# Turning C and two token blocks of x by transposing transfers on SP's queue, in place of VectorE's and TensorE's turnings

## Chip, cores and metric

The kernel runs on one core of a Trainium2 chip, in bfloat16 with float32 accumulation. The metric is the device time of one execution in microseconds (us), lower being better. The core has TensorE (PE, with its weight loads listed as PEld), VectorE (DVE), ScalarE (ACT), GpSimd (POOL) and SyncE (SP). SP computes nothing here: it issues transfers, which sixteen DMA engines carry out.

## What is computed

A gate mixes a state-space layer and a small feed-forward block over the same 2,048 tokens of 448 features. Cut to what matters:

```python
g = sigmoid((x * gate_w).sum(-1, keepdims=True))
# a: a complex diagonal recurrence over the tokens, state size 448
Lam_bar = exp(dt * Lam);  B_bar = ((Lam_bar - 1.0) / Lam)[:, None] * Bmat
Bu = einsum("bld,pd->blp", x, B_bar)
h[t] = Lam_bar * h[t - 1] + Bu[t]
a = 2.0 * einsum("blp,dp->bld", h, C_re + 1j * C_im).real + x * Dskip
# b: silu(x @ w1) @ w2, 448 -> 1792 -> 448
b = silu(x @ w1) @ w2
out = g * a + (1 - g) * b
```

TensorE contracts over the partitions (the 128 rows of on-chip memory), so three inputs that lie the other way round in DRAM have to be turned: x (tokens by features, needed as features by tokens), B, and C (outputs by states, needed as states by outputs).

## The kernel before

**Tiling.** The tokens are cut into four chunks of 512 (`tc` 0 to 3) and sixteen blocks of 128 (`tb` 0 to 15). The turned x stands in `xT[:, tc, q, :]` with four column groups `q` that start at features 0, 128, 256 and 320 (`XCOL`, the last two overlapping by 64). Each chunk goes through these products on PE: `F(tc)`, fourteen tiles x·w1 (line 711, weights `w1s`); `B(tc)`, seven tiles x·B (line 711, weights `BT`); `G(tb)`, the second feed-forward product (`ffn2`, line 822); and `C(tb)`, the read-out of the recurrence (`readout`, line 843, weights `CP`). F and B tiles go in pairs that hold two of the eight PSUM banks until ACT (lines 681 and 690) or DVE (line 688) has evicted them.

**The recurrence.** `lanes(tc)` runs on DVE: a rotation by COS and SIN, seven scans (line 784), a copy of the scans by POOL transfers, and a rotation back. The rotation back writes two products into `PO` (`"PO0"`, `"PO1"`) and leaves the result in `H[tc % 3]`, which `C` reads.

**Order.** PE runs in program order, which the bottom of the kernel writes by hand. For all other queues the class `Plan` simulates the program with costs and priorities given at each operation and fixes an order, so a planned cost sets an order and not a time. SP is one such queue: its transfers and the waits before them are carried out one after another in the planned order. `Waits` then places semaphore waits by the names that each operation reads and writes.

**How x is turned.** Chunk 0 is turned by PE at the start (line 504). For chunks 1, 2 and 3 `x_transposes` (line 536) lets PE turn the natural copy `xnat` with 32 small matmuls of 64 rows each into two banks; ACT and DVE (chunk 1) or ACT alone (chunks 2 and 3) copy the result into `xT` (lines 544 and 546). `x_blocks` is another way, by DVE, which `XBLK = ()` leaves unused.

**How C is turned.** `load_C` loads C by six transfers into `Cnat`, which lies in the buffer of `H[2]`, after POOL has zeroed a quarter of it (line 462). `readout_columns` turns 32 by 32 blocks on DVE (line 870, four instructions) into `UG[2]`, and sixteen transfers on SP (line 876) put the blocks where they belong in `CP`. Later `readout_weights(k)` scales these columns: two ACT copies with a scale into `ct` and two DVE instructions back into `CP` for k = 0 to 2 (lines 885, 886, 891, 894), and for the half-filled k = 3 two ACT copies of 64 partitions and one DVE instruction. `CTAT = 59.0` tells the planner not to place the ACT part earlier than that.

**Who evicts.** `UDVE = (0, 1, 4, 5, 6)` names the B tiles of chunk 0 that DVE evicts; ACT takes the pair (2, 3). `OUTA = tuple(range(4, 12))` names the blocks whose read-out is evicted by ACT into `ct` (line 848), added to `xnat` by a POOL transfer (line 850) and stored from there (line 851). The other blocks are evicted by one DVE instruction into one of five tiles `ot` (line 853) and stored from there (line 856).

**SP's queue at the start.** In planned order: x chunk 0, w1, B, the rest of w1, `gwb`, `dkb`, x chunk 1, the six loads of C, w2, x chunks 2 and 3, then the sixteen transfers of C's blocks; after these only stores.

The hand-written order of PE, which the steps below refer to:

```python
x_products(F(0, 0, NH) + B(0) + F(0, NH) + B(1), {..., XT1K: xt(1, XT1), 8: [lambda: lanes(0)] + [readout_columns] + ...}, [K - 2])
... G(0, 1, 2, 3) ... cp(0, 1, 2, 3)
x_products(F(1) + F(2, 0, 1) + B(2), {2: xt(2, "aa")} if 2 not in XBLK else {})
... G(4, 5, 6, 7)
x_products(F(2, 1) + B(3) + F(3), {1: xt(3, "aa") if 3 not in XBLK else [], 9: [lambda: gates(3)]})
C(0..3), lanes(3), C(4..7), G(8..13), C(8..11), G(14, 15), C(12..15)
```

Of the kernel before, what the change touches and what calls it, by code (L numbers as in the profile page):

```python
# [7 lines left out]
ALU = mybir.AluOpType  # L8
AF = mybir.ActivationFunctionType
# [20 lines left out]
XPRIO = {2: 15, 3: 20.2}  # L30
XBLK = ()
XBEH = {2: "PI_0", 3: "H0_0"}
UDVE = (0, 1, 4, 5, 6)
OUTA = tuple(range(4, 12))
PRMF = (1, 0)
PRMP = 9.7
CPRIO = 2.9
# [3 lines left out]
CBEH = ""  # L41
# [257 lines left out]
def bass_gated_mix__ssm_conv_s5__dense_activation_silu__prompt_kernel(nc, A_x, A_Lambda_re, A_Lambda_im, A_B_re, A_B_im, A_C_re, A_C_im,  # L299
               A_log_dt, A_Dskip, B_x, B_w1, B_w2, gate_w, out):  # L300
    with ExitStack() as ctx:
# [3 lines left out]
        def sb(name, shape, dtype):  # L305
            return E(nc.sbuf_tensor(name, list(shape), dtype))
# [15 lines left out]
        Cnat = H[2][:, :, :].rearrange("p s n -> p (s n)").rearrange("p (b l) -> p b l", b=4)  # L322
        cnn = [f"H2_{s}" for s in range(7)]
# [9 lines left out]
        ot = [sb(f"ot{k}", [128, D_MOD], BF16) for k in range(NOT)]  # L333
        ones = nc.const_aps.tensor(1.0, [128, 512], BF16)
# [40 lines left out]
        def sem():  # L375
            _s[0] += 1
            return E(nc.semaphore(name=f"d{_s[0]}"))
# [10 lines left out]
        def act_cost(n, aps=0):  # L388
            return 0.17 + n * 0.000833 + 0.09 * aps
# [4 lines left out]
        def ACT(fn, r, w, cost, prio, tag=""):  # L394
            return P.add("act", fn, r, w, cost, prio, tag=tag)

        def DVE(fn, r, w, cost, prio, tag=""):
            return P.add("dve", fn, r, w, cost, prio, tag=tag)

        def POOL(fn, r, w, cost, prio=10, tag=""):  # L400
            return P.add("pool", fn, r, w, cost, prio, tag=tag)
# [6 lines left out]
        def load(q, dst, src, name, nbytes, prio=None, after=()):  # L408
            nl[0] += 1
            prio = nl[0] if prio is None else prio  # L410
            P.add(q, lambda e: e.dma_start(dst, src), list(after), name.split(), 0.6 if q == "pool" else 0.5 if nbytes > 2000 else 0.35, prio, sem(), nbytes, tag="ld " + name)  # L411
# [32 lines left out]
        for dst, src, name in ((gwb, gate_w, "gwb"), (dkb, A_Dskip, "dkb")):  # L444
            load("sp", dst[:, :], src.rearrange("(o n) -> o n", o=1).partition_broadcast(128).rearrange("p o n -> p (o n)"),
                 name, 128 * 896)

        def load_xn(tc):
            load("sp", xnat[:, 4 * tc:4 * tc + 4, :],
                 x2[tc * CH:(tc + 1) * CH, :].rearrange("(b p) d -> p b d", p=128), f"xn{tc}", CH * 896)  # L450

        def load_C():

            n = 0
            for b0, b1, p in ((0, 3, 128), (3, 4, 64)):
                rows = lambda a: a[128 * b0:128 * b0 + p * (b1 - b0), :].rearrange("(b p) l -> p b l", p=p)
                for dst, src in (((0, 448), rows(A_C_re)), ((512, 896), rows(A_C_im[:, 0:384])), ((448, 512), rows(A_C_im[:, 384:448]))):
                    load("sp", Cnat[0:p, b0:b1, dst[0]:dst[1]], src, f"Cn{n}" + (" " + " ".join(cnn) if n == 0 else ""),
                         p * (b1 - b0) * max(300, 2 * (dst[1] - dst[0])), None, ["Cnz"] * b0)
                    n += 1  # L460

        POOL(lambda e: e.memset(Cnat[:, 3, :], 0.0), [], ["Cnz"], 0.9, 5)
        load_xn(1)
        load_C()
        load("sp", w2s[:, :, :], B_w2.rearrange("(fb p) d -> p fb d", p=128), "w2", F_FF * 896)
        load_xn(2)
# [55 lines left out]
        for tc in XBLK:  # L522
            xn_of[tc] = {q: [f"xT{tc}_{g}{m}" for g in range(4) for m in range(4)] for q in range(4)}
# [23 lines left out]

        def x_blocks(tc):


            X32 = (xT[:, 3, :, :] if tc == 2 else H[2][:, 0:4, :]).rearrange("p m (q b i) -> p m q b i", q=4, i=32)
            names = [f"XT{tc}2_{k}" for k in range(4)]
            held = cnn if tc == 3 else xn_of[3][0]
            xs = xnat[:, 4 * tc:4 * tc + 4, :]
            for k, (q0, q1, c, b0, b1) in enumerate(((0, 3, 0, 0, 2), (0, 3, 0, 2, 4), (3, 4, XCOL[3], 0, 2), (3, 4, XCOL[3], 2, 4))):
                n = q1 - q0
                src = xs[:, b0:b1, c:c + 128 * n].rearrange("p b (q m i) -> p b q m i", q=n, i=32)
                dst = X32.rearrange("p m q b i -> p b q m i")[:, b0:b1, q0:q1, :, :]
                DVE(lambda e, dst=dst, src=src: e.transpose(dst, src), [f"xn{tc}"] + names[0:k][0:1], [names[k]] + cnn * (tc == 3 and k == 0), 0.15 + 256 * n / 960, XPRIO[tc], "xTd")
            k = sem()  # L560
            for g in range(4):
                for m in range(4):
                    to = xT[32 * m:32 * m + 32, tc, :, :].rearrange("p q (b g i) -> p (q b) g i", b=4, i=32)[:, :, g, :]
                    P.add("sp", lambda e, to=to, g=g, m=m: e.dma_start(to, X32[32 * g:32 * g + 32, m, :, :, :].rearrange("p q b i -> p (q b) i")),
                          names + held, [f"xT{tc}_{g}{m}"], 0.68, 400, k, 150000, tag="xTm")
# [293 lines left out]
        ctn = [f"CT{g}{m}" for g in range(4) for m in range(4)]  # L859

        def readout_columns():

            C32 = UG[2][:, 0:NSLOT, :].rearrange("p s n -> p (s n)").rearrange("p (m t b i) -> p m t b i", m=4, b=4, i=32)
            names = [f"X32_{k}" for k in range(4)]
            held = [f"U2_{s}" for s in range(7)] + ["U2_3i"]
            turned = [f"BT{s}_{h}" for s in range(7) for h in range(2)]
            for b in range(4):
                src = Cnat[:, b, :].rearrange("p (t m i) -> p t m i", m=4, i=32)
                dst = C32.rearrange("p m t b i -> p b t m i")[:, b, :, :, :]
                DVE(lambda e, dst=dst, src=src: e.transpose(dst, src), [f"Cn{n}" for n in range(6)] + ["Cnz"] + [CBEH] * (CBEH != "") + cnn + turned, [names[b]],  # L870
                    0.15 + 896 / 960, CPRIO, "CTd")
            k = sem()
            for g in range(4):
                for m in range(4):
                    to = CP[32 * m:32 * m + 32, :, :].rearrange("p t (b g i) -> p (t b) g i", b=4, i=32)[:, :, g, :]
                    P.add("sp", lambda e, to=to, g=g, m=m: e.dma_start(to, C32[32 * g:32 * g + 32, m, :, :, :].rearrange("p t b i -> p (t b) i")),
                          names + held, [f"CT{g}{m}"], 0.75, 400, k, 300000, tag="CTm")

        def readout_weights(k):

            re, im = CP[:, k, 0:D_MOD], CP[:, 4 + k, 0:D_MOD] if k < 3 else None
            c, cn = ct[k % 2], f"ct{k % 2}"
            both = [cn + "a"]
            if k < 3:
                ACT(lambda e: e.activation(c[:, 0, :], im, AF.Copy, scale=sc2[:, k:k + 1]), ctn + ["sc2"], [cn + "a"], act_cost(448, 1), 8, "ct").at = CTAT
                ACT(lambda e: e.activation(c[:, 1, :], re, AF.Copy, scale=sc2[:, k:k + 1]), ctn + ["sc2"], [cn + "b"], act_cost(448, 1), 8, "ct").at = CTAT
                both.append(cn + "b")
            else:
                for a, b in ((slice(0, 64), slice(64, 128)), (slice(64, 128), slice(0, 64))):
                    ACT(lambda e, a=a, b=b: e.activation(c[a, 0, :], CP[b, 3, 0:D_MOD], AF.Copy, scale=sc2[b, 3:4]), ctn + ["sc2"], [cn + "a"], act_cost(448, 1), 8, "ct").at = CTAT  # L890
            DVE(lambda e: e.scalar_tensor_tensor(re, re, sc1[:, k:k + 1], c[:, 0, :], ALU.mult, ALU.add),
                ctn + ["sc1"] + both, [f"CP{k}"], 0.68, CPP, "CP")
            if k < 3:
                DVE(lambda e: e.scalar_tensor_tensor(im, im, nsc1[:, k:k + 1], c[:, 1, :], ALU.mult, ALU.add),
                    ctn + ["sc1"] + both, [f"CP{4 + k}"], 0.68, CPP, "CP")
# [20 lines left out]
        def xt(tc, who):  # L916
            return [lambda: x_transposes(tc, who)]
# [7 lines left out]
        def C(*tbs):  # L925
# [6 lines left out]
                   {PRMF: [parameters], (K - 2, 0): turn_b[:1], K - 2: turn_b[1:2], K - 1: turn_b[2:], XT1K: xt(1, XT1), 8: [lambda: lanes(0)] + [readout_columns] + [lambda tc=tc: x_blocks(tc) for tc in XBLK]}, [K - 2])  # L932
# [7 lines left out]
        x_products(F(1) + F(2, 0, 1) + B(2), {2: xt(2, "aa")} if 2 not in XBLK else {})  # L940
# [4 lines left out]
        x_products(F(2, 1) + B(3) + F(3), {1: xt(3, "aa") if 3 not in XBLK else [], 9: [lambda: gates(3)]})  # L945
# [40 lines left out]
```

## Time and profile before

| what | us |
|---|---|
| median of 3 runs (lowest, highest) | 140.45 (140.28, 141.47) |
| the profiled execution, device time | 140.08 |
| the profiled execution, span from first to last instruction | 138.3 |
| POOL busy | 46.4 |
| last PE instruction of the chain ends, from the span's start | 134.15 |
| mean granted TensorE clock | 0.998 of full speed |

The profile is of one execution; its times count from its first instruction. "Busy" is the time that an engine had an instruction running. The chain of waits follows the work that ended last back to its releaser at each step, so what stands in it sets the end. A group row gives a line, an engine, an operation, the shapes, the count, the total busy time and the mean in ns. The device time holds 1.8 us that lie outside the span.

### The profile page before, as it was taken

To read this page: it belongs to the slowest core of one execution; us is meant where nothing else is said; L and a number is where in the kernel's file an instruction comes from. 1 tells how busy PE (TensorE), PEld (TensorE's weight loads), DVE (VectorE), ACT (ScalarE), POOL (GpSimd) and SP (SyncE) were. 2 spreads that over 40 slices of the span, in tenths; PEclk is the share of its full clock that TensorE was granted. 3 is DMA by queue.
4 is the path that set the end of the run, shared out by engine and by line. 5 is a ranking of instruction groups with operands and counts; after the bars stand their busy time and mean duration, and the time that the engine had idled before them with its cause. 6 is when DMAs were issued, how large, how long until landed. Compare 5 with 4: busy or idle time off the path is not lost.

```text
span 138.3 us, 2881 instructions
## 1 busy us (share of the span) xinstructions
PE 134.7 (97%) x1137; PEld 66.0 (48%) x1137; DVE 119.3 (86%) x160; ACT 96.2 (70%) x167; POOL 46.4 (34%) x81
## 2 busy tenths in 40 slices
PE   7999999999999999999999999999999999999991
PEld 2545454445545444455454444445555555555561
DVE  0319999999999999999999999999999999992053
ACT  3259895999647999998299999899643149752200
POOL 7433030300548603067360030724063404374310
PEclk9999999999999999999999999999999999999999
DMA  4999999477859920029654010475459421379542
GB/s 140 324 355 292 270 364 341 63 102 83 96 77 155 158 40 19 24 37 160 93 87 64 0 38 0 65 120 81 114 106 159 102 33 18 51 100 151 118 102 68
DMA packets 33220, 16.48 MB, mean 119 GB/s; under 512 B 17075, under 2 KB 33078, under 8 KB 33206
## 3 DMA queue, kind: packets, MB, share of 16 engines
q0 software_dynamic: 7216, 6.43, 31.6%
q1 hardware_dynamic: 25440, 9.51, 25.8%
q10 hardware_dynamic: 550, 0.36, 0.8%
q8 instruction: 9, 0.15, 0.4%
q14 instruction: 5, 0.04, 0.1%
HBM read 7.11 MB, written 1.84 MB: 65 GB/s over the span
## 4 chain that ended last, share of the span: by engine, by line
PE 96%; DVE 1%; issue 0%; DVEq 0%
PE ps L711 46%; PE ps L822 31%; PE ps L843 14%; PE ps L489 2%; DVE ot L853 1%; PE ps L536 1%; PE ps L504 1%; PE ps L651 1%; PE ps L490 0%; PE ps L583 0%; PE ps L723 0%; DVEq L293 0%
## 5 line engine op out<-in xcount | busy, mean ns | idle before, releaser
L711 PE MATMUL ps<-xT,w1s 64*128 64x512 bf16 x392 | 48.2, 376 | 0.0
L822 PE MATMUL ps<-w2s,aT 128*128 128x448 bf16 x224 | 43.0, 353 | 0.0
L681 ACT ACTIVATE aT<-ps 128x1024 bf16<-128x1024 f32 (+1 forms) x30 | 28.9, 977 | 10.2 <-PE ps L711 10.1
L822 PEld LDWEIGHTS ps<-w2s,aT 128*128 128x128 bf16 x224 | 21.8, 98 | 20.9 <-issue 0.8
L711 PEld LDWEIGHTS ps<-xT,w1s 64*128 64x128 bf16 x392 | 19.6, 94 | 22.5 <-issue 1.2
L711 PE MATMUL ps<-xT,BT 64*128 64x512 bf16 x196 | 25.8, 376 | 0.0
L784 DVE TENSOR_TENSOR_SCAN Gf<-rc,gin,H 128x512 f32<-128x512 f32 x21 | 25.4, 1265 | 0.1
L830 POOL DMA_DIRECT2D xnat<-fe x16 | 14.4, 922 | 31.2 <-ACT fe L828 23.0
L843 PE MATMUL ps<-CP,H 128*128 128x448 bf16 (+2 forms) x126 | 21.7, 332 | 0.0
L411 POOL DMA_DIRECT2D UG<-Gf x27 | 15.7, 660 | 15.7 <-DVE Gf L784 15.4
L828 ACT ACTIVATE fe<-ps,g 128x448 bf16<-128x448 f32 x16 | 9.9, 627 | 11.1 <-PE ps L822 8.1
L843 PEld LDWEIGHTS ps<-CP,H 128*128 128x128 bf16 x126 | 11.6, 98 | 10.0 <-DVE xnat L752 0.4
L711 PEld LDWEIGHTS ps<-xT,BT 64*128 64x128 bf16 x196 | 10.8, 94 | 11.2 <-DVE Gf L609 0.2
L752 DVE TENSOR_TENSOR H<-UG,COS 128x3584 bf16<-128x3584 bf16 (+2 forms) x9 | 16.1, 1810 | 0.0
L411 POOL DMA_DIRECT2D UG<-UG x8 | 4.5, 567 | 27.1 <-ACT UG L690 27.1
L690 ACT ACTIVATE UG<-ps 128x1024 bf16<-128x1024 f32 (+1 forms) x13 | 11.8, 936 | 0.5 <-PE ps L711 0.5
L853 DVE SCALAR_TENSOR_TENSOR ot<-ps,g,xnat 128x448 bf16<-128x448 f32 (+2 forms) x10 | 5.7, 584 | 7.5 <-issue 6.2
L913 ACT ACTIVATE xnat<-xnat,g 128x448 bf16<-128x448 bf16 x16 | 9.7, 663 | 0.1
L906 ACT ACTIVATE junk<-xg 128x448 bf16<-128x448 bf16 x16 | 9.6, 598 | 0.1
L850 POOL DMA_DIRECT2D xnat<-ct x8 | 6.9, 864 | 6.7 <-ACT ct L848 6.6
L848 ACT ACTIVATE ct<-ps,g 128x448 f32<-128x448 f32 x8 | 5.1, 633 | 5.7 <-PE ps L843 5.7
L752 DVE TENSOR_TENSOR PI<-UG,SIN 128x1536 bf16<-128x1536 bf16 (+1 forms) x8 | 8.5, 1083 | 0.0
(99 smaller groups left out, 123.8 us busy)
## 6 DMA issues: line engine op xcount, KB each, us to landing
UG<-Gf POOLq DMA_DIRECT2D x21, 128.0 KB, 2.8
xnat<-fe POOLq DMA_DIRECT2D x16, 112.0 KB, 2.6
w2s<-in_B_w_dram SPq DMA_DIRECT2D x1, 1568.0 KB, 8.5
xnat<-in_A_x_dram SPq DMA_DIRECT2D x3, 448.0 KB, 8.2
CP<-UG SPq DMA_DIRECT2D x16, 56.0 KB, 2.4
xnat<-ct POOLq DMA_DIRECT2D x8, 112.0 KB, 2.9
out_dram<-xnat SPq DMA_DIRECT2D x8, 112.0 KB, 2.3
out_dram<-ot SPq DMA_DIRECT2D x7, 112.0 KB, 1.8
```

Of the source, the lines that this page charges most:

```text
L411: P.add(q, lambda e: e.dma_start(dst, src), list(after), name.split(), 0.6 if q == "pool" else 0.5 if nbytes > 2000 else 0.35, prio, sem() ...
L681: ACT(lambda e, src=src, dst=dst: e.activation(dst, src(), AF.Silu), [tk, "tbl"], [f"aT{tc % 2}_{m}" for m in names], act_cost(512 * n), 2 ...
L690: ACT(lambda e, src=src, dst=dst: e.activation(dst, src(), AF.Copy), [tk], after, act_cost(512 * n), 5, "U")
L711: r = pe.matmul(bk(toks[k], b), weights(tile, p0, p0 + 64, i), xT[p0:p0 + 64, tc, i, :], start=(h == 0 and n == 0), stop=(h == 1 and n == 2))
L752: DVE(lambda e: e.tensor_tensor(o, a, b, op), r, w, dve_cost(n, 2), prio, tag)
L784: DVE(lambda e, s=s, b=b, init=init: e.tensor_tensor_scan(Gf[:, s, :], rc[:, b:b + 1].to_broadcast([128, CH]), A[:, s, :], init, ALU.mult, ...
L822: r = pe.matmul(bk(tk)[:, 0:D_MOD], aT[tc % 2][:, fb, o:o + 128], w2s[:, fb, :], start=(fb == 0), stop=(fb == NFB - 1))
L828: ACT(lambda e: e.activation(f[:, :], bk(tk)[:, 0:D_MOD], AF.Copy, scale=g1[:, tb:tb + 1]), [tk, f"g1_{tc}"], [fn], act_cost(448, 1), 7, "fe")
L830: P.add("pool", lambda e: e.dma_start(Tb[:, tb, :], f[:, :], accum_op=ALU.add), [fn, f"Tb{tb}"], [f"Tb{tb}"], 0.94, 2, sem(), 250000, tag= ...
L843: r = pe.matmul(bk(tk)[:, 0:b - a], H[tc % 3][:, s, o:o + 128], CP[:, s, a:b], start=(s == 0), stop=(s == NSLOT - 1))
L906: ACT(lambda e, tb=tb, b=b: e.activation(junk[:, :], xg[:, b, :], AF.Copy, accum_out=zl[:, tb:tb + 1]), ["xg"], ["junk", f"zl{tc}"], act_c ...
L913: ACT(lambda e, tb=tb: e.activation(Tb[:, tb, :], xnat[:, tb, :], AF.Copy, scale=g[:, tb:tb + 1]), [f"xd{tc}", f"g_{tc}"], [f"Tb{tb}"], ac ...
```

## The change

C's four pieces and x's chunks 2 and 3 are written turned, straight from DRAM, by `dma_start_transpose` on SP's queue. `load_C`, `readout_columns`, the zeroing of `Cnat`, `x_blocks` and the PE turnings of chunks 2 and 3 go; the natural copies of x stay, since the gates read them. `turn_x(2)` and `turn_C` stand in SP's queue behind w2 and ahead of the natural loads of chunks 2 and 3; `turn_x(3)` waits for the name `"PO1"`, which `lanes(0)` writes. C's last columns are no longer packed into the two halves of `CP[:, 3, :]`: the imaginary part goes to a tile of its own, `C3`, which is the fifth `ot` tile, and `readout_weights(3)` combines the halves with two DVE instructions. `UDVE` gains the pair (2, 3), so DVE evicts all of chunk 0's B tiles, and `OUTA` shrinks to blocks 8 to 11, so DVE evicts the read-outs 4 to 7.

```diff
-XPRIO = {2: 15, 3: 20.2}
-XBLK = ()
-UDVE = (0, 1, 4, 5, 6)
-OUTA = tuple(range(4, 12))
+XDMA = (2, 3)
+XAFT = ["PO1"]
+UDVE = (0, 1, 2, 3, 4, 5, 6)
+OUTA = (8, 9, 10, 11)
...
+        C3, c3n = ot[NOT - 1], " ".join(f"ot{NOT - 1}{m}" for m in range(3))
...
+        def turn(dst, src, name, nbytes, cost, after=()):
+            nl[0] += 1
+            P.add("sp", lambda e: e.dma_start_transpose(dst, src), list(after), name.split(), cost, nl[0], sem(), nbytes, tag="ldT " + name)
+
+        def turn_x(tc, after=()):
+            for c, n in ((0, 3), (3, 1)):
+                turn(xT[:, tc, c:c + n, :], x2[tc * CH:(tc + 1) * CH, XCOL[c]:XCOL[c] + 128 * n], " ".join(f"xT{tc}_{q}" for q in range(c, c + n)), CH * 256 * n, 2.6 if n == 3 else 1.3, after)
+
+        def turn_C():
+            for k, a in enumerate((A_C_re, A_C_im)):
+                turn(CP[:, 4 * k:4 * k + 3, 0:D_MOD], a[:, 0:384], " ".join(f"CT{4 * k + m}" for m in range(3)), 448 * 768, 1.5)
+                turn((CP[:, 3, 0:D_MOD], C3[:, :])[k][:, None, :], a[:, 320:448], "CT3" if k == 0 else c3n, 448 * 256, 1.6)
...
-        POOL(lambda e: e.memset(Cnat[:, 3, :], 0.0), [], ["Cnz"], 0.9, 5)
-        load_xn(1)
-        load_C()
+        if 1 not in XDMA:
+            load_xn(1)
         load("sp", w2s[:, :, :], B_w2.rearrange("(fb p) d -> p fb d", p=128), "w2", F_FF * 896)
+        if 2 in XDMA:
+            turn_x(2)
+        turn_C()
...
         load_xn(2)
         load_xn(3)
...
         def readout_weights(k):
...
+            up = slice(64, 128)
             if k < 3:
...
+                re, im, rn, mn = CP[:, k, 0:D_MOD], CP[:, 4 + k, 0:D_MOD], f"CT{k}", f"CT{4 + k}"
+                a, to = slice(0, 128), ((CP[:, k, 0:D_MOD], re, sc1, [f"CP{k}", rn], 0), (CP[:, 4 + k, 0:D_MOD], im, nsc1, [f"CP{4 + k}", mn], 1))
             else:
...
+                re, im, rn, mn = CP[up, 3, 0:D_MOD], C3[up, :], "CT3", c3n
+                a, to = up, ((CP[0:64, 3, 0:D_MOD], re, nsc1, ["CP3"], 0), (CP[up, 3, 0:D_MOD], im, sc1, ["CP3", rn], 1))
...
+            for dst, src, f, w, n in to:
+                DVE(lambda e, dst=dst, src=src, f=f, n=n: e.scalar_tensor_tensor(dst, src, f[a, k:k + 1], c[a, n, :], ALU.mult, ALU.add),
+                    ([rn] if n == 0 else mn.split()) + ["sc1", cn + "ab"[n]], w, 0.68, CPP, "CP")
...
-                   {..., XT1K: xt(1, XT1), 8: [lambda: lanes(0)] + [readout_columns] + [lambda tc=tc: x_blocks(tc) for tc in XBLK]}, [K - 2])
+                   {..., XT1K: xt(1, XT1) if 1 not in XDMA else [], 8: [lambda: lanes(0)] + [lambda: turn_x(3, XAFT)] * (3 in XDMA and bool(XAFT))}, [K - 2])
...
-        x_products(F(1) + F(2, 0, 1) + B(2), {2: xt(2, "aa")} if 2 not in XBLK else {})
+        x_products(F(1) + F(2, 0, 1) + B(2), {2: xt(2, "aa")} if 2 not in XDMA else {})
...
-        x_products(F(2, 1) + B(3) + F(3), {1: xt(3, "aa") if 3 not in XBLK else [], 9: [lambda: gates(3)]})
+        x_products(F(2, 1) + B(3) + F(3), {1: xt(3, "aa") if 3 not in XDMA else [], 9: [lambda: gates(3)]})
```

More of the change, by code (lines that the diff above doesn't have):

```diff
@@ L29 @@
 XT1 = "da"
-XPRIO = {2: 15, 3: 20.2}
-XBLK = ()
-XBEH = {2: "PI_0", 3: "H0_0"}
-UDVE = (0, 1, 4, 5, 6)
-OUTA = tuple(range(4, 12))
+XDMA = (2, 3)
+XAFT = ["PO1"]
+UDVE = (0, 1, 2, 3, 4, 5, 6)
+OUTA = (8, 9, 10, 11)
 PRMF = (1, 0)
 PRMP = 9.7
-CPRIO = 2.9
 CPP = 20.5
@@ L40 @@
 GPR = (14, 20.3, 21.5, 19)
-CBEH = ""
 CASTB = (360000, 360000, 360000)
@@ L321, in bass_gated_mix__ssm_conv_s5__dense_activation_silu__prompt_kernel @@
         H = [sb(f"H{k}", [128, NSLOT, CH], BF16) for k in range(3)]
-        Cnat = H[2][:, :, :].rearrange("p s n -> p (s n)").rearrange("p (b l) -> p b l", b=4)
-        cnn = [f"H2_{s}" for s in range(7)]
         COS = sb("COS", [128, NSLOT, CH], BF16)
@@ L443, in bass_gated_mix__ssm_conv_s5__dense_activation_silu__prompt_kernel, with load_xn @@
         load_w1("sp", len(w1cuts) - 2, 2, 4)
+        def load_xn(tc):
+            load("sp", xnat[:, 4 * tc:4 * tc + 4, :],
+                 x2[tc * CH:(tc + 1) * CH, :].rearrange("(b p) d -> p b d", p=128), f"xn{tc}", CH * 896)
+        def turn(dst, src, name, nbytes, cost, after=()):
[8 more added lines that the diff above has]
+                turn((CP[:, 3, 0:D_MOD], C3[:, :])[k][:, None, :], a[:, 320:448], "CT3" if k == 0 else c3n, 448 * 256, 1.6)
+        if 1 in XDMA:
+            turn_x(1)
         for dst, src, name in ((gwb, gate_w, "gwb"), (dkb, A_Dskip, "dkb")):
@@ L446, in bass_gated_mix__ssm_conv_s5__dense_activation_silu__prompt_kernel @@
                  name, 128 * 896)
[L448 to L460, printed above, removed]
-        POOL(lambda e: e.memset(Cnat[:, 3, :], 0.0), [], ["Cnz"], 0.9, 5)
-        load_xn(1)
-        load_C()
-        load("sp", w2s[:, :, :], B_w2.rearrange("(fb p) d -> p fb d", p=128), "w2", F_FF * 896)
+        if 1 not in XDMA:
+            load_xn(1)
+        load("sp", w2s[:, :, :], B_w2.rearrange("(fb p) d -> p fb d", p=128), "w2", F_FF * 896)
+        if 2 in XDMA:
+            turn_x(2)
+        turn_C()
+        if 3 in XDMA and not XAFT:
+            turn_x(3)
+        if 1 in XDMA:
+            load_xn(1)
         load_xn(2)
@@ L521, in bass_gated_mix__ssm_conv_s5__dense_activation_silu__prompt_kernel @@
         xn_of = {tc: {q: [f"xT{tc}_{h}" for h in range(2)] for q in range(4)} for tc in range(1, NCH)}
-        for tc in XBLK:
-            xn_of[tc] = {q: [f"xT{tc}_{g}{m}" for g in range(4) for m in range(4)] for q in range(4)}
+        for tc in XDMA:
+            xn_of[tc] = {q: [f"xT{tc}_{q}"] for q in range(4)}
         xn_of[0] = {q: [f"xT0_{q}{part}{h}" for part in range(2) for h in range(2)] for q in range(4)}
@@ L546, in x_transposes @@
                     ACT(lambda e, src=src, dst=dst: e.activation(dst, src(), AF.Copy), [tk], [f"xT{tc}_{h}"], act_cost(1024), 2.2, "xTe")
[L548 to L565, printed above, removed]
         cosn = [f"COS{k}" for k in range(4)] + ["COSd"]
@@ L857, in readout @@
                       [f"ot{tb % NOT}{n}"], [], 0.3, 1, outs[tb % NOT], 128 * 2 * (b - a), tag="st")
[L859 to L877, printed above, removed]
@@ L879, in readout_weights @@
         def readout_weights(k):
-            re, im = CP[:, k, 0:D_MOD], CP[:, 4 + k, 0:D_MOD] if k < 3 else None
             c, cn = ct[k % 2], f"ct{k % 2}"
-            both = [cn + "a"]
+            up = slice(64, 128)
             if k < 3:
-                ACT(lambda e: e.activation(c[:, 0, :], im, AF.Copy, scale=sc2[:, k:k + 1]), ctn + ["sc2"], [cn + "a"], act_cost(448, 1), 8, "ct").at = CTAT
-                ACT(lambda e: e.activation(c[:, 1, :], re, AF.Copy, scale=sc2[:, k:k + 1]), ctn + ["sc2"], [cn + "b"], act_cost(448, 1), 8, "ct").at = CTAT
-                both.append(cn + "b")
-            else:
-                for a, b in ((slice(0, 64), slice(64, 128)), (slice(64, 128), slice(0, 64))):
-                    ACT(lambda e, a=a, b=b: e.activation(c[a, 0, :], CP[b, 3, 0:D_MOD], AF.Copy, scale=sc2[b, 3:4]), ctn + ["sc2"], [cn + "a"], act_cost(448, 1), 8, "ct").at = CTAT
@@ L891, in readout_weights @@
[L891 to L895, printed above, removed]
+                re, im, rn, mn = CP[:, k, 0:D_MOD], CP[:, 4 + k, 0:D_MOD], f"CT{k}", f"CT{4 + k}"
+                a, to = slice(0, 128), ((CP[:, k, 0:D_MOD], re, sc1, [f"CP{k}", rn], 0), (CP[:, 4 + k, 0:D_MOD], im, nsc1, [f"CP{4 + k}", mn], 1))
+            else:
+                re, im, rn, mn = CP[up, 3, 0:D_MOD], C3[up, :], "CT3", c3n
+                a, to = up, ((CP[0:64, 3, 0:D_MOD], re, nsc1, ["CP3"], 0), (CP[up, 3, 0:D_MOD], im, sc1, ["CP3", rn], 1))
@@ new lines, in readout_weights @@
+            ACT(lambda e: e.activation(c[a, 0, :], im, AF.Copy, scale=sc2[a, k:k + 1]), mn.split() + ["sc2"], [cn + "a"], act_cost(448, 1), 8, "ct").at = CTAT
+            ACT(lambda e: e.activation(c[a, 1, :], re, AF.Copy, scale=sc2[a, k:k + 1]), [rn, "sc2"], [cn + "b"], act_cost(448, 1), 8, "ct").at = CTAT
+            for dst, src, f, w, n in to:
+                DVE(lambda e, dst=dst, src=src, f=f, n=n: e.scalar_tensor_tensor(dst, src, f[a, k:k + 1], c[a, n, :], ALU.mult, ALU.add),
+                    ([rn] if n == 0 else mn.split()) + ["sc1", cn + "ab"[n]], w, 0.68, CPP, "CP")
@@ L931, in bass_gated_mix__ssm_conv_s5__dense_activation_silu__prompt_kernel @@
         x_products(F(0, 0, NH) + B(0) + F(0, NH) + B(1),
-                   {PRMF: [parameters], (K - 2, 0): turn_b[:1], K - 2: turn_b[1:2], K - 1: turn_b[2:], XT1K: xt(1, XT1), 8: [lambda: lanes(0)] + [readout_columns] + [lambda tc=tc: x_blocks(tc) for tc in XBLK]}, [K - 2])
+                   {PRMF: [parameters], (K - 2, 0): turn_b[:1], K - 2: turn_b[1:2], K - 1: turn_b[2:], XT1K: xt(1, XT1) if 1 not in XDMA else [], 8: [lambda: lanes(0)] + [lambda: turn_x(3, XAFT)] * (3 in XDMA and bool(XAFT))}, [K - 2])
         gates(0)
```

## The prediction

> **What bounds the kernel now.** I read the page's head first, for which engine is full; columns are busy time, share of the span and instructions.
>
> ```profile
> span 138.3 us, 2881 instructions
> PE 134.7 (97%) x1137; PEld 66.0 (48%) x1137; DVE 119.3 (86%) x160; ACT 96.2 (70%) x167; POOL 46.4 (34%) x81
> ```
>
> A busy PE may still be a waiting one, so next the chain of waits in order of time (start, us, what). From 0.78 to 134.15 every piece is PE's; here are those around the turnings that go.
>
> ```profile
> 38.83 5.50 PE ps L711 x50
> 44.33 0.47 PE ps L536 x32
> 44.80 11.22 PE ps L711 x104
> ...
> 70.71 0.47 PE ps L536 x32
> 71.18 21.80 PE ps L711 x202
> ...
> 134.15 0.03 issue
> ```
>
> The two turnings stand in the chain with 0.47 us each. The pace of line 711 is the same with and without a turning before it (11.22 / 104 and 21.80 / 202 both give 0.108 us), so PE waits for nothing around them. The list of waits confirms it: ACT waited 10.1 us for line 711, and no PE matmul for an eviction. Then I read the groups that the change touches (count, busy us, mean ns, idle before):
>
> ```profile
> L870 DVE STREAM_TRANSPOSE UG<-H 128x896 bf16<-128x896 bf16 x4 | 4.2, 1077 | 0.0
> L688 DVE CAST UG<-ps 128x1024 bf16<-128x1024 f32 x2 | 2.4, 1211 | 0.0
> L853 DVE SCALAR_TENSOR_TENSOR ot<-ps,g,xnat 128x448 bf16<-128x448 f32 x7 | 4.7, 677 | 7.5 <-issue 6.2 <-PE ps L843 1.3
> L891 DVE SCALAR_TENSOR_TENSOR CP<-CP,sc1s,ct 128x448 bf16<-128x448 bf16 x4 | 2.7, 666 | 0.0
> ```
>
> **PE.** Two turnings of 32 matmuls go: 2 x 0.47 = 0.94 us, all of it on the path. Nothing is added to PE, and its written order is otherwise the same. This is the whole gain that the chain offers; what follows asks whether anything takes it back.
>
> **DVE.** It loses 4 x 1.08 = 4.3 us of block turning. It gains the pair (2, 3), 1.21; four read-outs, 4 x 0.677 = 2.71; and an eighth instruction on CP, 0.67: 4.59 in all, so +0.3 us. Its last rotation ends at 125.38 in the timeline, and the matmuls that read it, C(12), start at 130.00. With PE 0.94 earlier 3.7 us of cover are left, so +0.3 costs nothing. Without that cover it would cost its 0.3 us. In time the shift is early: 4.3 less and 1.21 more before 25 us let the first rotation start up to 3 us sooner, and the read-outs give 2.7 of it back after 98 us. A read-out can wait behind a DVE instruction of at most 2.0 us (line 752, 3,584 elements), while PE makes one each 1.34 us and has eight banks, so none fills them.
>
> **ACT and POOL.** ACT loses four copies of x (line 546, 4 x 1.02), one pair (1.02) and four read-outs (4 x 0.63): 7.6 us. POOL loses the zeroing (0.84) and four accumulating transfers (4 x 0.86 to issue). Neither is in the chain: worth nothing, but ACT gets slack.
>
> **SP's queue and the transfers.** Six loads of C and sixteen moves of C's blocks go; eight transposing transfers come. The trace of before has none, so I bound their pace. The fast end is the plain loads, 302 GB/s at a DMA share of 0.92; the slow end is the only transfers here that rearrange, the sixteen moves of 56 KB in runs of 64 bytes. They take 0.917 MB from 24.51 to 38.5 (the last issue at 36.1 plus 2.4), 65 GB/s, with 0.66 us of SP for each and with free DMA time left. Below: the windows (PE, PEld, DVE, ACT, POOL busy, clock, DMA share, GB/s) and the queue (start, us).
>
> ```profile
> 20.00:25.00 5.00, 5.00 (x50) 2.28 (x48) 5.00 (x7) 3.11 (x6) 0.00 (x0) 1.00 0.92 302
> 24.50:38.50 14.00, 14.00 (x90) 6.86 (x86) 13.97 (x26) 12.05 (x25) 2.89 (x4) 1.00 0.68 86
> ```
>
> ```profile
> 24.51 12.23 SPq L876 DMA_DIRECT2D CP<-UG  x16
> ```
>
> I take 65, since turning is rearranging; both ends stay. w2, issued at 14.83, landed 8.5 us later at 23.3. With C's 0.80 MB gone from ahead of it, at 302 GB/s, it lands about 2.7 us sooner, at 20.6, and then x chunk 2 (512 x 512 x 2 bytes, 0.524 MB) takes 8.0 us at 65 GB/s (1.7 at 302), to 28.6. C (2 x 448 x 512 x 2 bytes, 0.918 MB) takes 14.1 (3.0), to 42.7; the natural chunks 2 and 3 behind it, 0.92 MB, 3.1, to 45.8. Who waits:
>
> ```profile
> 49.17 0.38 PE L711 MATMUL ps<-xT,BT 64*128 64x512 bf16 x1
> ...
> 75.55 0.38 PE L711 MATMUL ps<-xT,BT 64*128 64x512 bf16 x1
> 75.61 0.95 DVE L752 TENSOR_TENSOR PO<-UG,SIN 128x1536 bf16<-128x1536 bf16 x1
> ```
>
> PE first needs chunk 2 at 49.17 less 0.47, 48.7: spare 20 us. ACT first reads C at 59.99 (line 885): spare 17. DVE reads the natural chunk 2 at 70.90, or up to 3 us sooner: spare 22. Chunk 3 waits on SP for `"PO1"`, which DVE writes until 49.61 (or up to 3 us sooner). Behind that wait SP holds only the stores, from 96.60 on. The transfer then takes 8.0 us, to 57.6. PE needs it at 75.55 less 0.94, 74.6; and DVE's next write of `"PO1"`, at 75.61 or up to 3 us sooner, now waits for it too: spare 15 at least. So the transfers cost nothing at either end, and what the cover is worth stands under the rivals. Chunk 1's natural load keeps its place (issued at 8.40, landed 7.4 later at 15.8; PE turns it at 17.79). What comes behind it is now w2 and not C; were the engines shared evenly between the two, its 0.459 MB would take 1.5 us more, to 17.3, still in time. Freed DMA time before 20 us bounds a gain there at nothing, since PE waits for no load after its start.
>
> The Trainium skill ("VectorE: DVE Perf Modes", The three transpose paths) speaks against the change: it gives 390 ns for TensorE's turning of a 128x128 block and 1309 ns for the DMA crossbar's. This trace has 16 such blocks turned by PE in 0.47 us of its time, 0.03 us each, so I read the page's figures as latencies of one block alone, and not as paces that add up. "DMA: Bandwidth & Descriptors" (Bandwidth) gives 261 GB/s for transposing transfers, by which, as an estimate from that page, chunk 2 would land in 2.0 us and the sum would stay as it is. No run shown here has either.
>
> **Sum.** The profiled execution took 140.08, of it 138.3 of span and 1.8 around it: 140.08 - 0.94 = 139.14. It lies 0.37 under the median of the three runs. I start from the median of all four executions, (140.28 + 140.45) / 2 = 140.37, and get 139.4 us, 0.67% less. A change of about 1% (1.4 us) is what a measurement of this kernel can tell from none.
>
> **Rivals.**
>
> *A: the transposing transfers are late and become the bound.* They run one after another on one queue, so what decides is their pace. All 1.97 MB and the 3.1 us of natural loads must be through from 20.6 to 74.6, which needs 1.97 / 50.9 us = 39 GB/s; below that PE stands before chunk 3 (C is late for ACT below 1.33 MB / 39.4 us = 34 GB/s). For it: pieces of two bytes are smaller than the 64-byte runs that gave 65. Against: those left DMA time free and were held by their own issue. At half of 65 the transfers need 60.5 us, end at 84.2, and PE is 9.6 us late: 149.0 us. Chance 0.08. By the skill's 1309 ns for each of the 60 blocks, one after another (an estimate from that page), it would be 78.5 us and a time near 167.
>
> *B: the crowd.* Between 39 and 99 GB/s (1.44 MB from 20.6 to 35.3) the transfers still run while POOL adds the first feed-forward results into `xnat`, and ACT waits for these.
>
> ```profile
> 38.71 0.63 ACT L828 ACTIVATE fe<-ps,g 128x448 bf16<-128x448 f32 x1 [2.00 <-DMA xnat<-fe]
> 40.30 0.63 ACT L828 ACTIVATE fe<-ps,g 128x448 bf16<-128x448 f32 x1 [0.96 <-DMA xnat<-fe]
> ```
>
> ACT then evicts F(1) from 41.35, and PE takes its fifth bank pair near 44.9, when the first must be free (42.4), so ACT may be 2.5 us later than now. If the two accumulations that it waits for take twice their 2.6 us to land, ACT is 5.2 later and PE loses 2.7: 142.1. Against: C's sixteen moves crowd the same time in before, at a share of 0.68, and ACT has more slack in after. It decides from 2.5 us on. Chance 0.10.
>
> *C: the removed turnings filled time in which PE would have waited.* Then 140.4. Against: equal pace on both sides of them, and no wait of PE. Chance 0.08, with the cases in which a little of B eats the gain.
>
> *D: more than the chain shows*, some 1.5 us less, 138.9 or below, by better order on ACT and DVE or by spread between runs (0.4 between the profile and the median). Nothing in the chain offers it. Chance 0.08.
>
> **How the numbers follow.** The forecast has the remaining 0.66. Faster by over 1%: D, 0.08. Slower by over 1%: A, B, and 0.02 for an order of the planner's that I can't see, 0.20. Within 1%: 0.72. The range goes from 138.6, the forecast less the spread and a part of D, to 142.2, which takes in B. Outside are A and the ends of B and D. The forecast with C alone would span 138.8 to 140.6.
>
> **What would show it.** Right: no line 536 for chunks 2 and 3 in the chain, PE's last piece ending near 133.2, line 711 at 0.108 us throughout, SP's transposing transfers landed before 48.7, 60 and 74.6, DVE's last rotation before 129. Wrong: PE or its weight loads idle behind a transfer into `xT` (A), ACT waiting for `xnat<-fe` over 5 us (B), DVE ending past 129, or PE's gain there but the tail after it longer than 4.2 us.

## The result, and the profile after

| | before | after |
|---|---|---|
| median of 7 runs (lowest, highest), us | 140.31 (140.22, 141.47) | 139.31 (139.04, 139.69) |
| ratio to before, 95% interval | | 0.9917 (0.9888 to 0.9946) |
| the profiled execution, us | 140.08 | 139.69 |
| its span, us | 138.3 | 137.9 |

The forecast was 139.4 us, 0.67% less; measured are 139.31 us and 0.83% less, with an interval that holds the forecast. Here and below the medians are of all executions, while the ratios are of the fast ones (without those over 1.5% above the fastest of their kernel, one each of before, late_x3 and b_too) and are not the quotients of the medians. By the medians the change is 1.00 us, 0.71%. A second comparison on another chip (below) gave 0.9932 (0.9912 to 0.9951), by the medians 1.04 us. The profiled execution after happens to be the slowest of its seven, which matters for reading it. First the head of the page after (busy, share of the span, instructions), then its chain of waits in order of time.

```profile
span 137.9 us, 2723 instructions
PE 134.3 (97%) x1073; PEld 65.5 (47%) x1073; DVE 119.8 (87%) x162; ACT 89.5 (65%) x158; POOL 42.3 (31%) x76
```

```profile
5.07 4.13 PE ps L701 x30
9.19 0.18 PE ps L573 x4
...
39.38 16.73 PE ps L701 x154
56.10 10.70 PE ps L812 x56
66.80 25.79 PE ps L701 x238
```

Two pieces of the chain of before that stand beside these readings:

```profile
4.95 3.69 PE ps L711 x30
66.72 3.99 PE ps L711 x36
```

The two pieces of line 545 (536 before) that stood at 44 and 71 us are gone, and the x·w1 and x·B products now run as one piece in each stage: 5.50 + 0.47 + 11.22 = 17.19 us have become 16.73, and 3.99 + 0.47 + 21.80 = 26.26 have become 25.79. That is 0.46 + 0.47 = 0.93 us. The span shows only 0.4 of it, and the first line says why: the thirty matmuls of line 701 (711 before) at the start took 4.13 us, 3.69 in before. There PE waits for the first pieces of w1, which both kernels load alike; in no_turn below the chain itself goes through their transfer, `DMA w1s<-in_B_w_dram`, for 5.55 us. Over all profiled executions of this study PE came to line 573 (583 before), the parameter matmuls, between 8.50 and 9.93 us; a kernel that shares these instructions with before had 9.93 and before itself 8.57. So one profile can't give a difference below a microsecond by its span; its stages can. Behind them nothing changed: from the first matmul of C(12) to the end of the span it is 8.29 us in before and 8.28 in after.

SP's queue after, as the timeline has it (start, us, what), and a window of five microseconds (engines' busy time, clock, DMA share, GB/s). The share adds up the times of packets and passes 1 where these overlap:

```profile
8.73 0.51 SPq L407 DMA_DIRECT2D w2s<-in_B_w_dram  x1
9.28 11.54 SPq L447 DMA_TRANSPOSE xT<-in_A_x_dram  x2
20.87 3.70 SPq L447 DMA_TRANSPOSE CP<-in_A_C_re_dram  x2
24.61 1.44 SPq L447 DMA_TRANSPOSE CP<-in_A_C_im_dram  x1
26.09 1.26 SPq L447 DMA_TRANSPOSE ot<-in_A_C_im_dram  x1
27.39 1.34 SPq L407 DMA_DIRECT2D xnat<-in_A_x_dram  x2
48.27 2.75 SPq L447 DMA_TRANSPOSE xT<-in_A_x_dram  x2
```

```profile
20.00:25.00 5.00, 5.00 (x50) 2.24 (x46) 5.00 (x17) 4.09 (x7) 0.22 (x1) 1.00 1.20 171
```

w2 landed 12.1 us after its issue, at 20.8; chunk 2's two pieces by 24.8, C's last by 30.0, chunk 3's by 53.0. So x's chunk 2 and C, 1.44 MB, took the 9.2 us from 20.8 to 30.0: 157 GB/s. Their packets in the trace run from 17.2 to 29.2, and 0.15 MB of them ended ahead of 20.8; the other 1.29 MB give 154 GB/s. The window has 171 GB/s at a DMA share of 1.20, with the end of w2 in it, where before had 302 at 0.92. Per byte that is 2.3 times the share, 1.6 times in pace below (184 at 0.90); but all of it was there 20 us and more before PE or ACT asked. Chunk 2's pair also held SP for 11.54 us, which the prediction did not count.

### The profile page after: what moved, and what is told of

It reads as the page before. It is cut to its first block, busy times and chain, and to the rows that moved or that the text cites. A ratio compares the mean times of both kernels' runs of the same rounds, so it can differ in the third digit from the quotient of the medians.

```text
span 137.9 us, 2723 instructions
## 1 busy us (share of the span) xinstructions
PE 134.3 (97%) x1073; PEld 65.5 (47%) x1073; DVE 119.8 (87%) x162; ACT 89.5 (65%) x158; POOL 42.3 (31%) x76
## 4 chain that ended last, share of the span: by engine, by line
PE 97%; DVE 0%; issue 0%
PE ps L701 47%; PE ps L812 31%; PE ps L833 15%; PE ps L498 2%; PE ps L513 1%; PE ps L641 1%; PE ps L545 0%; DVE ot L843 0%; PE ps L713 0%; PE ps L499 0%; PE ps L573 0%
## 5 line engine op out<-in xcount | busy, mean ns | idle before, releaser
L701 PEld LDWEIGHTS ps<-xT,w1s 64*128 64x128 bf16 x392 | 20.2, 95 | 23.1 <-issue 1.5
L407 POOL DMA_DIRECT2D UG<-Gf x27 | 15.5, 597 | 16.0 <-DVE Gf L774 15.8
L701 PEld LDWEIGHTS ps<-xT,BT 64*128 64x128 bf16 x196 | 10.8, 94 | 11.2 <-DVE Gf L599 0.2
L843 DVE SCALAR_TENSOR_TENSOR ot<-ps,g,xnat 128x448 bf16<-128x448 f32 (+2 forms) x14 | 8.2, 611 | 5.9 <-issue 4.6
L680 ACT ACTIVATE UG<-ps 128x1024 bf16<-128x1024 f32 (+1 forms) x12 | 10.3, 922 | 0.0
L742 DVE TENSOR_TENSOR PO<-UG,SIN 128x1536 bf16<-128x1536 bf16 (+1 forms) x8 | 8.6, 1082 | 0.0
L742 DVE TENSOR_TENSOR H<-H,PI 128x3584 bf16<-128x3584 bf16 x4 | 8.1, 2022 | 0.1
## 6 DMA issues: line engine op xcount, KB each, us to landing
w2s<-in_B_w_dram SPq DMA_DIRECT2D x1, 1568.0 KB, 12.1
```

The costliest lines, as they stand in the source:

```text
L680: ACT(lambda e, src=src, dst=dst: e.activation(dst, src(), AF.Copy), [tk], after, act_cost(512 * n), 5, "U")
L701: r = pe.matmul(bk(toks[k], b), weights(tile, p0, p0 + 64, i), xT[p0:p0 + 64, tc, i, :], start=(h == 0 and n == 0), stop=(h == 1 and n == 2))
L742: DVE(lambda e: e.tensor_tensor(o, a, b, op), r, w, dve_cost(n, 2), prio, tag)
```

## The experiments

All stand against before, run beside them on the same chip. "F(1)" and "F(2)" are the stages from the first matmul of F(1) or F(2) to the next block of another kind, read off the starts of the PE matmuls of one profiled execution, to 0.01 us. Twelve executions stand behind most medians, four behind late_x3 and three_again, six behind three.

| run | median us (before) | ratio (95% interval) | F(1) | F(2) |
|---|---|---|---|---|
| before | | | 17.19 | 26.26 |
| after | 139.31 (140.31) | 0.9917 (0.9888 to 0.9946) | 16.73 | 25.79 |
| no_turn | 139.74 (140.61) | 0.9935 (0.9906 to 0.9964) | 16.73 | 25.79 |
| x_only | 139.99 (140.61) | 0.9945 (0.9909 to 0.9981) | 16.73 | 25.79 |
| c_only | 141.21 (140.61) | 1.0051 (1.0010 to 1.0091) | 17.19 | 26.60 |
| old_evict | 139.95 (140.61) | 0.9931 (0.9902 to 0.9959) | 16.73 | 25.79 |
| three | 139.13 (140.26) | 0.9906 (0.9871 to 0.9940) | 16.72 | 25.79 |
| late_x3 | 142.56 (140.26) | 1.0115 (1.0047 to 1.0184) | 16.73 | 28.00 |
| no_wait | 139.52 (140.26) | 0.9938 (0.9911 to 0.9965) | 16.73 | 25.79 |
| pace | 139.24, one run | | 16.73 | 25.79 |
| after_again | 139.36 (140.40) | 0.9932 (0.9912 to 0.9951) | 16.73 | 25.79 |
| three_again | 138.55 (140.40) | 0.9876 (0.9862 to 0.9891) | 16.73 | 25.79 |
| b_too | 140.73 (140.40) | 1.0028 (1.0009 to 1.0048) | 16.72 | 25.79 |
| c_new | 140.32 (140.40) | 1.0000 (0.9984 to 1.0016) | 17.19 | 26.26 |

### Which part of the change gains

The limits in us of the next expectations were set for a before of 140.3 to 140.4. Beside the first four runs it took 140.61, so the ratios and the stages decide; a limit in us would have to lie 0.2 to 0.3 higher.

**no_turn** takes the turnings away and puts nothing in their place: a bound on what any other way of turning these chunks could gain.

```diff
-r = pe.matmul(..., xT[p0:p0 + 64, tc, i, :], ...)
+r = pe.matmul(..., xT[p0:p0 + 64, min(tc, 1), i, :], ...)
-x_products(F(1) + F(2, 0, 1) + B(2), {2: xt(2, "aa")} ...)
+x_products(F(1) + F(2, 0, 1) + B(2), {})
-x_products(F(2, 1) + B(3) + F(3), {1: xt(3, "aa") ..., 9: ...})
+x_products(F(2, 1) + B(3) + F(3), {9: ...})
```

> The kernel before without PE's turnings of chunks 2 and 3 and without their four evictions; nothing takes their place, and the products of these chunks read the turned chunk 1, so the output isn't the reference's. Theory (PE is the bound, only its two turnings of 0.47 us count): 0.94 us under before, 139.4. Rival 1 (freeing DVE and ACT of C's turning gives a part of the gain): less than the change gained, 139.8 or more. Rival 2 (the transposing transfers cost something that eats a part of a larger gain): under the changed kernel, 138.9 or less.

0.65% less, 0.91 us, and the same two stages as the changed kernel to 0.01 us. By the stages neither rival holds: the whole gain is there without C, and the transfers take nothing from it. The times by themselves can't tell 0.91 us from the 0.95 to 1.16 of the change.

**x_only** is before with `turn_x(2)` ahead of the natural loads of chunks 2 and 3 and `turn_x(3, ["PO1"])` after `lanes(0)`; C stays on DVE.

> The kernel before with x's chunks 2 and 3 turned by the transposing transfers, C still turned by DVE and sixteen moves. Theory: 139.4, the whole gain. Rival 1 (C's side gives a part): 139.8 or more. Rival 2 (the transfers cost something): above the kernel that leaves the turnings out.

0.55% less, 0.77 us. The stages are those of after; the median is 0.25 over no_turn, inside both intervals. The profile has a place for it behind the stages: from the first matmul of C(12) to the end of the span it is 8.63 us here and 8.28 in no_turn. What made that tail longer isn't shown; no transfer into `xT` runs then.

**c_only** is the other half: C by transfers, x by PE, evictions as before.

```diff
-XDMA = (2, 3)
-UDVE = (0, 1, 2, 3, 4, 5, 6)
-OUTA = (8, 9, 10, 11)
+XDMA = ()
+UDVE = (0, 1, 4, 5, 6)
+OUTA = tuple(range(4, 12))
```

> The changed kernel with C turned by the transposing transfers, but x's chunks 2 and 3 turned by PE as before, and with the evictions shared as before. Theory: C's turning stands beside PE's work, so 140.3, no change from before. Rival 1: 139.9 or less. If the transfers of C crowd the queue, above 140.6.

0.51% slower, 0.72 us, which the theory had at nothing; 141.21 us lies past the 140.6 that the expectation gave to a crowd on the queue. F(2) is 0.34 us longer, with a gap of 0.52 us between two matmuls' starts at 74.44. The chain of waits of this kernel leaves PE just there:

```profile
70.46 1.01 DVE xg L742
71.47 0.02 issue
71.49 0.67 ACT junk L874 x2
72.16 0.91 ACT aT L671
73.07 1.84 ACT xT L555 x2
74.91 0.05 issue
74.96 18.95 PE ps L701 x174
```

The new planned order put a gate's sum (`junk`) on ACT ahead of an eviction (`aT`). The sum had to wait for DVE's `xg`, the eviction and both copies of chunk 3 queued behind it, and PE waited for the last copy. None of it is a transfer of C. It is a price of PE's turning that the trace of before did not show: the turning needs two evictions, of 1.0 us each, in time. These 0.34 us are about half of the loss. In the profile the tail from C(12) is longer as well, 8.83 us against 8.29, and there one store held SP for 1.02 us in place of 0.43; whether the other executions lost the rest there is open.

**c_new** is c_only with the evictions of the changed kernel, thus with another planned order.

> C by transposing transfers, x's chunks 2 and 3 turned by PE, with the evictions of the changed kernel in place of those of before. Theory (the kernel with the old evictions lost 0.4 us because its planned order put a gate's sum ahead of an eviction on ACT while PE's turning held two banks): no gap of PE there, 140.3 as before. Rival (C's transfers themselves cost it): 140.8 as with the old evictions.

1.0000 (0.9984 to 1.0016), F(2) is back at 26.26, and the tail is 8.23 us. C's transfers cost nothing and gain nothing; what c_only lost came with its evictions and the order planned for them. This run changes more of the order than the one sum, so the sum's part is read from the chain and not isolated.

**old_evict** is the changed kernel with `UDVE` and `OUTA` of before.

> The changed kernel with the evictions of before (ACT takes the B pair (2, 3) of chunk 0 and the read-outs 4 to 7). Theory: neither engine bounds, so 139.3 as the changed kernel. Rival 1: if the new share between DVE and ACT is a part of the gain, 139.6 or more.

0.69% less, 0.97 us, beside 0.9932 for the changed kernel in after_again: the share of the evictions is worth nothing that shows. The 139.95 us lie past the rival's 139.6, and just past it with the slower before counted in; but the stages are those of after, and the tail from C(12) is 0.20 longer in the profile, 8.48 us.

### Whether the transfers are near the path

**pace** puts three more transposing transfers (0.917 MB into `H[2]`, free until `lanes(2)`) behind chunk 3's.

```diff
+def more():
+    for tc, c, n, d in ((0, 0, 3, 0), (0, 3, 1, 3), (1, 0, 3, 4)):
+        turn(H[2][:, d:d + n, :], x2[tc * CH:(tc + 1) * CH, XCOL[c]:XCOL[c] + 128 * n], ..., ["PO1"])
```

> The changed kernel with three more transposing transfers behind chunk 3's, 0.917 MB into a buffer that is free until lanes(2), so that five of them (1.44 MB) run one after another beside little other traffic: measures their pace. Theory: the time stays at 139.3 and the five land within 8 to 11 us of the first issue (about 130 to 180 GB/s, as behind w2). Rival (64-byte runs set the pace, 65 GB/s): 22 us, landed after 70.

The queue and two windows of this kernel:

```profile
47.81 2.74 SPq L447 DMA_TRANSPOSE xT<-in_A_x_dram  x2
50.59 4.41 SPq L447 DMA_TRANSPOSE H<-in_A_x_dram  x3
```

```profile
50.00:52.00 2.00, 2.00 (x22) 0.88 (x18) 2.00 (x2) 1.93 (x7) 0.00 (x0) 1.00 0.90 184
52.00:54.00 2.00, 2.00 (x22) 0.90 (x20) 2.00 (x3) 1.98 (x4) 0.60 (x2) 1.00 1.01 200
```

The fifth, issued at 53.5, landed 5.1 us later at 58.6: 1.44 MB in 10.8 us from the first issue, 133 GB/s with the latency of the first and last in it, and 184 and 200 GB/s in the two windows, at a DMA share of 0.90 and 1.01. The 65 GB/s of the moves in runs of 64 bytes was no bound for these. The time stayed at 139.24.

**no_wait** sets `XAFT = []`, so that chunk 3's turning follows C's, issued at 27.04.

> The changed kernel without the wait for PO1: chunk 3's turning follows C's on SP's queue, ahead of the natural loads of chunks 2 and 3, and shares the DMA engines with POOL's accumulations from 33 us on. Theory: nothing on PE's path waits for these, so 139.3 as the changed kernel. Rival (rival B of the prediction, the crowd): ACT waits longer for xnat<-fe than the 0.85 us of the changed kernel, and over 2.5 us more of it shows as time: 139.8 or more.

0.62% less, inside the interval of the changed kernel. From the list of waits of no_wait (us in total, times, longest):

```profile
ACT fe L818 <- DMA xnat<-fe: 1.7, 2, 0.9
```

The changed kernel has 1.7 there too, and before had 3.0. Chunk 3's last piece landed at 33.8 and the natural loads behind it at 36.3, while POOL issued the first accumulation at 35.40. So even here the two hardly met: the transfers are too quick for a crowd, and the wait for `"PO1"` is not needed for the time. What a real crowd would cost was not tried.

**late_x3** moves chunk 3's turning behind `lanes(1)` and lets it wait for `"gin"`.

```diff
-8: [lambda: lanes(0)] + [lambda: turn_x(3, XAFT)] * ...
+8: [lambda: lanes(0)]
...
 lanes(1)
+turn_x(3, ["gin"])
```

> The changed kernel, but chunk 3's turning waits for lanes(1)'s last small result, which DVE writes near 72.5, in place of lanes(0)'s product near 48. Landed 4.7 us after its issue it comes near 77.3, and PE needs it near 75.2. Theory: what is late on the path costs PE its lateness one to one, 2.1 us: 141.4. Rival: the planned order hides it or the late evictions behind it add to it: under 140.3, or over 142.5.

```profile
PEld ps L701 <- DMA xT<-in_A_x_dram: 2.5, 1, 2.5
```

The transfers were issued at 72.50 and the last landed at 77.1; the weight loads waited 2.5 us for it, and F(2) is 28.00 us long, 2.20 more than in after. So the pace is hidden by time and not by anything else: late transfers do reach PE, about one to one. The profiled execution took 141.75. Of the four executions two, 141.30 and 141.75, fit the theory's 141.4; the other two, 143.37 and 143.55, lie past the rival's 142.5, and so, just, does the median of all four, 142.56. What these two lost beyond the 2.2 us no profile shows. That stays open.

### Going further

**three** and **three_again** (the same kernel) turn chunk 1 by transfers as well: `XDMA = (1, 2, 3)`, which issues `turn_x(1)` behind the last of w1. **after_again** is the changed kernel run once more beside the second of them. The three expectations follow in the order three, after_again, three_again.

> The changed kernel with chunk 1 turned by transposing transfers as well, issued behind the last of w1. Theory: a third turning of 0.47 us leaves PE's path, so 0.47 us under the changed kernel, 138.8 where that is 139.3 (ratio to before 0.989). By the pace of the changed kernel (0.524 MB in 3.9 us behind what is ahead of it) chunk 1 lands near 18 and PE needs it near 22.6; w2 would land near 24 and PE needs it at 28.1. Rival (rival A of the prediction, the transfers are late): PE waits before B(1) or before the first G, and the time is 139.5 or more.

> The changed kernel once more, beside the next two on one chip. Theory: 0.94 us under before. Rival (the 1.16 us of the first comparison was more than PE's two turnings): 1.2 us or more.

> Chunk 1 turned by transfers too, once more, beside the changed kernel. Theory: 0.47 us under the changed kernel (1.41 under before). Rival (the earlier transfers make PE wait for w1 or x at the start, which gives the gain back): as the changed kernel, within 0.2 us.

The first comparison gave 0.9906 with an interval that holds the theory's 0.989 and the changed kernel's 0.9917: undecided. Its profiled execution reached the parameter matmuls only at 9.55. The second, beside the changed kernel, decides, though with four executions: 0.9876 (0.9862 to 0.9891) against 0.9932 (0.9912 to 0.9951), 1.74 us and 0.95 us under before. The trace gives the cleaner number. From the parameter matmuls to the first G are 19.49 us in before, after and no_turn, and 19.02 in both profiles of this kernel: 0.47 us, the third turning. In the chain of three_again the products of the first stage run in one piece from 13.34 on, with no turning at 18:

```profile
12.99 0.35 PE ps L641 x24
13.34 14.24 PE ps L701 x132
27.59 10.70 PE ps L812 x56
```

The time gained, 0.79 more than the change, is over 0.47; how much of the rest is the start, which came early here (parameter matmuls at 8.50), the runs can't tell. Chunk 1's first piece landed at 7.20 + 8.0 = 15.2 us (15.5 in three). This version, 138.55 us, beats both kernels.

**b_too** turns B by six transfers as well, loads all of w1 ahead of it and orders F(0) ahead of B(0) on PE.

```diff
-load("sp", Bnat[...], ...)  # four loads
+for p, rows, c0, a in (("r", slice(0, 448), 0, A_B_re), ("t", slice(384, 448), 448, A_B_im), ("i", slice(0, 384), 512, A_B_im)):
+    turn(BT[:, 0:3, c0:c0 + r], a[rows, 0:384], ...)
+    turn(BT[:, 3:4, c0:c0 + r], a[rows, 320:448], ...)
-x_products(F(0, 0, NH) + B(0) + F(0, NH) + B(1), ...)
+x_products(F(0) + B(0) + B(1), ...)
```

> Chunks 1 to 3 of x, C and also B by transposing transfers, all of w1 loaded ahead of B, and PE's written order F(0), B(0), B(1) so that B is needed later (near 15.5 us). Theory: B's three turnings of 0.23, 0.23 and 0.35 us leave PE's path too, 0.81 us under the kernel with three chunks, 2.2 us under before, 138.1. At 140 to 150 GB/s B lands by 16 and w2 by 25.5; PE needs w2 near 26.5. Rival (transfers late): PE waits before B(0) or the first G, and the time is over 139.

0.28% slower than before. PE did wait, but not for B. The chain:

```profile
16.70 1.26 SPq L441
17.96 0.04 issue
18.00 4.81 DMA gwb<-in_gate_w_dram
...
22.93 1.09 DVE xg L741
24.03 1.15 DVE UG L677
25.17 0.05 issue
25.22 3.84 PE ps L700 x34
```

`gwb`, the gate's row, stands behind eight transposing transfers in SP's queue, was issued at 18.00 (7.20 in before) and landed at 22.8. DVE's `xg` waited for it 2.56 us, an eviction of B queued behind `xg`, and PE had no banks: gaps of 0.47 and 1.76 us between starts, at 20.17 and 23.46. From the parameter matmuls to the first G it took 20.03 us, 19.02 in three_again; without the 2.0 us that the two gaps hold beyond the usual 0.11 between starts it would be 18.0, an estimate by which B's turnings had left the path. Loading `gwb` and `dkb` ahead of B was not tried, so whether B's 0.81 us can be had is open.

## Why the prediction was right, point by point

- **What bounds the kernel.** Right, and the size too: 0.94 us from the two pieces in the chain, 0.93 in the stages after, 0.91 for the kernel without them (ratio 0.9935), 0.95 and 1.16 by the ratios of the change in two comparisons, 1.04 and 1.00 by their medians.
- **DVE.** Forecast +0.3 us of work with 3.7 us of cover. Busy time rose by 0.5 (119.3 to 119.8) and the last rotation ended at 126.60, 3.0 us before C(12) at 129.61, where 3.4 were forecast. The cover held; old_evict shows that the share of evictions does not matter.
- **ACT and POOL.** Forecast 7.6 us less on ACT; 6.7 measured (96.2 to 89.5), worth nothing in time as said.
- **The pace of the transfers.** The term that was mis-sized: 65 GB/s taken, 157 measured in its place. The row I called nearest was held by its own sixteen issues of 0.66 us, as the prediction itself said of it. The miss cost nothing, since even 65 left 15 us of cover. w2 was forecast at 20.6 and landed at 20.8.
- **SP's issue.** Missed: the first transposing transfer behind w2 held SP for 10.2 us. In this change only C's transfers and the natural loads of chunks 2 and 3 stood behind it (these issued at 27.39 and not at 15.47, first read at 69.75). In b_too the issues of eight such transfers, 1.24 to 2.70 us each, put off `gwb` and turned a gain into a loss.
- **Rival A (late).** Not so at this pace, but the mechanism is real: late_x3 lost what it was late, 2.2 us in its profile.
- **Rival B (the crowd).** Not so: the prediction let it decide between 39 and 99 GB/s (98 by its own 1.44 MB in 14.7 us); at 157 C had landed at 30.0, before POOL's accumulations began, and ACT's wait for these fell from 3.0 to 1.7 us. no_wait, with chunk 3 ahead of them as well, has the same 1.7.
- **Rival C (PE would have waited anyway).** Not so in this change. c_only shows the opposite case: with PE turning x, another order of ACT makes PE lose 0.34 us at the turning.
- **Rival D (over 1%).** Not so: 0.83% and 0.68%. The first interval reaches 1.12%, the second ends at 0.88%.
- **The planner's order.** The prediction gave 0.02 to an order that it couldn't see. The changed kernel shows no cost of it; but c_only lost 0.34 us at PE's turning, and the tails of x_only, old_evict and c_only are 0.2 to 0.5 us longer in their profiles. Nothing in the prediction says why the changed kernel's order had neither, so that part was luck.
- **The signs.** Chunk 2, C and chunk 3 had landed at 24.8, 30.0 and 53.0, ahead of the 48.7, 60 and 74.6 that were named, and line 701 ran at 0.108 to 0.109 us a matmul. PE's last piece did not end near 133.2 but at 135.12. The start came 0.55 us later in this execution, and the chain now follows PE to its last matmul: the last piece has the 42 of C(12) to C(15), where in before it left PE after the 21 of C(12) to C(14). Measured to the same place, PE's last matmul ended at 135.11 after and 135.49 before.
- **The figures of the Trainium skill.** The 1309 ns per block of the Trainium skill ("VectorE: DVE Perf Modes", The three transpose paths) are no pace here: 1.44 MB are 44 blocks of 128x128, which took 10.8 us in pace, 0.25 us each. The 261 GB/s that the Trainium skill ("DMA: Bandwidth & Descriptors", Latency and other measured facts) gives for transposing transfers with a non-contiguous middle dimension were not reached, where 133 to 200 GB/s were measured.

## What to carry to other kernels

Where the chain of waits is one engine from start to end, as in this kernel, a change is worth what it takes off that engine, piece by piece as the chain prices it; what it takes off the others is slack, as long as their new order opens no gap (c_only). Compare stages and not spans of single profiles when a start of loads varies by more than the gain. And before putting slow-to-issue transfers on a queue, list what stands behind them and which engine's own queue will stop for it: a 112 KB row held up an eviction and with it the engine that mattered.

## What the hardware showed that was not expected

- The first transposing transfer behind a long load held SP far longer than its own issue: 10.25 us for the first of chunk 2 behind w2, until 1.3 us before w2 landed, and 5.63 us in x_only, until 2.3 us before; with little ahead of them (chunk 3's, and those of pace) it was 1.25 to 1.55 us. Plain loads are held too, but less: chunk 2's natural load behind w2 took SP 2.30 us in before (two loads in 3.30). Why isn't shown.
- Transposing transfers one after another moved 184 and 200 GB/s at a DMA share of 0.90 and 1.01 (pace), some 60 to 66% of the 302 GB/s of plain loads at 0.92.
- PE reached the same instruction between 8.50 and 9.93 us in executions whose instructions are the same up to it, by the arrival of the first pieces of w1; this spread is larger than the change.
